# Decode attention with an MLP on one core: K transposed by VectorE in 32x32 blocks instead of by TensorE, and output sums spread over four quadrants

## The chip, the cores and the metric

The kernel runs on one core of a Trainium2 chip. Times are device microseconds of that core. The profile is one execution taken by the hardware profiler; its span is some 2 us shorter than the timed run.

## The reference

One decode step of four sequences: 32 query heads over 16 K/V heads, the last 2048 positions of the cache, and an MLP block on the same input, all added up.

```python
B, Sq, D = x.shape                    # 4, 1, 576
Hq, Dh = 32, 128
Hkv, Sk = k_cache.shape[1], k_cache.shape[2]     # 16, 8192
W = min(4096, max(256, Sk // 4))      # 2048
q = (x @ wq).reshape(B, Sq, Hq, Dh).transpose(0, 2, 1, 3)
k = jnp.repeat(k_cache[:, :, Sk - W:, :], rep, axis=1)     # rep = 2
v = jnp.repeat(v_cache[:, :, Sk - W:, :], rep, axis=1)
p = softmax(einsum("bhqd,bhkd->bhqk", q, k) * Dh ** -0.5)
o = einsum("bhqk,bhkd->bhqd", p, v)
attention = o.transpose(...).reshape(B, Sq, Hq * Dh) @ wo
# second branch; with one position the shifted h is zero, so x1 = x:
mlp = x + gelu(layernorm(x) @ w3) @ w4
# x above is the layernorm of the input; output: input + attention + mlp
```

What matters is the traffic: K and V of 16 heads are 2 MB each, with the weights 87.2 MB in all, and every byte is used once.

## The kernel before

All four sequences of one K/V head are one tile: partition p*4+b holds 64 consecutive positions of sequence b. TensorE transposes K in 128x128 chunks (64 per head), ScalarE and VectorE evict them (copy them from PSUM to SBUF), and each chunk then gives scores for the 8 queries of its head. Columns of the other sequences are masked.

```python
kvp = ...tile_pool(name="kv", bufs=NKV)             # NKV = 7, loads of K and V in one order
ps_tp, ps_s: 2 PSUM buffers each; ps_o, ps_m, ps_acc: 1
accB = AB[0:B, 448:448 + NB_]                       # 64 columns
accA = accA_t[0:B, :]                               # 512 columns, partitions 0 to 3
# ... cuts ...
def acc_matmuls(lhsT, rhs):                         # used by o_proj and mlp_out
    nc.tensor.matmul(out=accA, lhsT=lhsT, rhs=rhs[:, 0:NA], start=first, ...)
    nc.tensor.matmul(out=accB, lhsT=lhsT, rhs=rhs[:, NA:D], start=False, ...)

def k_transpose(h, g):                              # g: eight groups of 8 chunks
    tp = ps_tp.tile([P, GC, P], BF16, tag="tp")
    for i in range(GC):
        nc.tensor.transpose(out=tp[:, i, :], in_=kn[:, g * GC + i, :], identity=ident_bf[:])
    # ScalarE (g in 0,2,3,5,6) or VectorE copies tp to kt in SBUF

def k_scores(h, g):
    for i in range(GC):
        nc.tensor.matmul(out=S_ps[h][:, g * GC + i, :], lhsT=kt[:, i, :], rhs=q, start=True, stop=True)

# softmax of a head, one head behind the scores:
#   sm_max    VectorE maximum over the free axis of S
#   sm_maxT   TensorE transpose of it, mask, maximum, diagonal
#   sm_sub    "shift": TensorE spreads the maximum over all partitions; VectorE subtracts: T = S - m
#   sm_exp    one ScalarE exponential of 128 x 512
#   sm_den    VectorE sum of 128 x 512;  sm_rden: TensorE sum over partitions, reciprocal
def pv(h, g):                                       # two heads behind (LAG = 2)
    for c in range(g * GC, (g + 1) * GC):
        nc.tensor.matmul(out=o, lhsT=vn[:, c, :], rhs=PT[h][:, c, :], ...)

for t in range(Hkv + LAG + 1):                      # one step per head
    for g in range(NGR):
        k_transpose(t, g); k_scores(...); pv(t - LAG, g); o_proj(t - LAG - 1)  # and the softmax of t - 1
        # at t == 7: mlp_g, 180 matmuls
for lo, hi in zip(W4_PIECES, W4_PIECES[1:]):
    mlp_out(lo, hi)                                 # 36 "output steps", w4 is loaded last
```

## Time and profile before

| | |
|---|---|
| time, median of 3 runs | 241.27 us (237.99 to 242.65) |
| span of the profiled run (which took 240.92 us) | 239.1 us |
| TensorE busy | 189.5 us (79%) |
| VectorE / ScalarE busy | 95.9 / 55.8 us |
| loaded | 87.2 MB, at about 420 GB/s while it flows |

First the page of the kernel before. The first line below gives busy time, share and instructions of each engine; the others cut the span into 40 slices, with the busy tenths of TensorE, the TensorE clock that the profile shows as granted (9 is 90% or more) and the DMA engines' share.

```profile
PE 189.5 (79%) x3641; PEld 167.9 (70%) x3641; DVE 95.9 (40%) x226; ACT 55.8 (23%) x98; POOL 2.4 (1%) x12
...
PE   0544996999922492999997999989799998894994
...
PEclk9999999569975587696555556999869999955589
DMA  6999999999999999999999969999999999980000
```

The loads flow for 36 slices of 6 us and then stop; the last four slices, some 24 us, are a tail of TensorE work. So two things matter: how long the loads take, and what still has to be done when they end.

The groups of the kernel before: line, engine, operation, result and operands, shapes, count, then busy us and the mean ns of one.

```profile
L235 PE MATMUL tp<-ident_bf,kn 128*128 128x128 bf16 x1024 | 95.2, 248 | 10.8 <-DMA kn<-in_A_k_cache_dram 8.7
...
L240 ACT COPY kt<-tp 128x512 f32<-128x512 f32 x80 | 46.8, 586 | 149.2 <-PE tp L235 149.1
L242 DVE COPY kt<-tp 128x512 int32<-128x512 int32 x48 | 32.9, 686 | 63.8 <-PE tp L235 62.1
...
L286 DVE TENSOR_REDUCE dp<-pt 128x8 f32<-128x512 bf16 x16 | 17.4, 1090 | 15.1 <-ACT pt L281 15.1
```

K's transposes are the largest group of TensorE. A busy share of 79% does not say that they set the time: the timeline has to show that.

The timeline of the kernel before (start, duration, engine, line, operation), cut to the shift matmul of head 14, the projections of two heads and two of the output steps. Each output step is a pair, 512 columns and 64.

```profile
202.61 0.38 PE L222 MATMUL accA_t<-wo_sb,on 128*4 128x512 bf16 x1
...
202.85 0.38 PE L222 MATMUL accA_t<-wo_sb,on 128*4 128x512 bf16 x1
...
207.74 0.38 PE L271 MATMUL mb<-dg,ones_f 8*128 8x8 f32 x2
...
224.82 0.61 PE L222 MATMUL accA_t<-w_sb,gT 128*4 128x512 bf16 x1
...
225.30 0.61 PE L222 MATMUL accA_t<-w_sb,gT 128*4 128x512 bf16 x1
```

A step from 224.82 to 225.30 takes 0.48 us, twice the 0.24 us of the same shape at 202.6. The 576 columns of a step then pass at 1.2 per nanosecond instead of 2.4: TensorE runs at half its clock here.

### The profile page before, as it was taken

To read this page: it belongs to the slowest core of one execution; us is meant where nothing else is said; L and a number is where in the kernel's file an instruction comes from. 1 tells how busy PE (TensorE), PEld (TensorE's weight loads), DVE (VectorE), ACT (ScalarE), POOL (GpSimd) and SP (SyncE) were. 2 spreads that over 40 slices of the span, in tenths; PEclk is the share of its full clock that TensorE was granted. 3 is DMA by queue.
4 is the path that set the end of the run, shared out by engine and by line. 5 is a ranking of instruction groups with operands and counts; after the bars stand their busy time and mean duration, and the time that the engine had idled before them with its cause. 6 is when DMAs were issued, how large, how long until landed. Compare 5 with 4: busy or idle time off the path is not lost.

```text
span 239.1 us, 7840 instructions
## 1 busy us (share of the span) xinstructions
PE 189.5 (79%) x3641; PEld 167.9 (70%) x3641; DVE 95.9 (40%) x226; ACT 55.8 (23%) x98; POOL 2.4 (1%) x12
## 2 busy tenths in 40 slices
PE   0544996999922492999997999989799998894994
PEld 0433986988921392889996998888788987873441
DVE  5024264536530052352324444564425656544001
ACT  2000352324300041130021131342223433211000
POOL 3000000000000000000000000000000000000000
PEclk9999999569975587696555556999869999955589
DMA  6999999999999999999999969999999999980000
GB/s 234 422 436 433 392 419 425 411 426 423 434 417 419 423 394 425 425 423 419 433 419 391 426 255 430 397 408 422 407 401 423 425 433 410 419 349 8 3 0 2
DMA packets 10688, 87.67 MB, mean 367 GB/s; under 512 B 792, under 2 KB 4896, under 8 KB 5408
## 3 DMA queue, kind: packets, MB, share of 16 engines
q1 hardware_dynamic: 10656, 87.18, 88.1%
q8 instruction: 28, 0.46, 0.8%
q14 instruction: 4, 0.03, 0.0%
HBM read 87.17 MB, written 0.00 MB: 365 GB/s over the span
## 4 chain that ended last, share of the span: by engine, by line
PE 47%; DMA 39%; DVE 7%; issue 3%; ACT 2%; SPq 0%; DVEq 0%
DMA vn<-in_A_v_cache_dram 28%; PE tp L235 17%; DMA kn<-in_A_k_cache_dram 8%; PE accA_t L222 8%; PE O L302 6%; PE S L251 5%; PE AB L323 4%; DMA wq_sb<-in_A_wq_dram 3%; DVE dp L286 2%; PE mb L271 2%; PE dn L291 2%; ACT pt L281 1%; PE AB L223 1%; ACT kt L240 1%; DVE junk L262 1%
## 5 line engine op out<-in xcount | busy, mean ns | idle before, releaser
L235 PE MATMUL tp<-ident_bf,kn 128*128 128x128 bf16 x1024 | 95.2, 248 | 10.8 <-DMA kn<-in_A_k_cache_dram 8.7
L235 PEld LDWEIGHTS <-kn 128*128 128x128 bf16 x1024 | 74.4, 113 | 16.5 <-DMA kn<-in_A_k_cache_dram 9.0
L240 ACT COPY kt<-tp 128x512 f32<-128x512 f32 x80 | 46.8, 586 | 149.2 <-PE tp L235 149.1
L242 DVE COPY kt<-tp 128x512 int32<-128x512 int32 x48 | 32.9, 686 | 63.8 <-PE tp L235 62.1
L302 PE MATMUL O<-pt,vn 128*128 128x8 bf16 x1024 | 43.6, 167 | 13.9 <-DMA vn<-in_A_v_cache_dram 9.2
L251 PE MATMUL S<-qT,kt 128*128 128x8 bf16 x1024 | 46.3, 169 | 0.0
L302 PEld LDWEIGHTS <-vn 128*128 128x128 bf16 x1024 | 35.3, 99 | 15.1 <-DMA vn<-in_A_v_cache_dram 9.4
L251 PEld LDWEIGHTS <-kt 128*128 128x128 bf16 x1024 | 43.5, 102 | 0.5 <-issue 0.5
L286 DVE TENSOR_REDUCE dp<-pt 128x8 f32<-128x512 bf16 x16 | 17.4, 1090 | 15.1 <-ACT pt L281 15.1
L222 PE MATMUL accA_t<-wo_sb,on 128*4 128x512 bf16 x32 | 14.1, 503 | 0.3 <-DVE on L308 0.3
L262 DVE TENSOR_TENSOR junk<-mxT,maskT 8x128 f32<-8x128 f32 x16 | 4.5, 278 | 22.3 <-PE mxT L260 22.3
L323 PE MATMUL AB<-ln2T,w_sb 128*128 128x4 bf16 x144 | 11.8, 202 | 0.0
L323 PEld LDWEIGHTS <-w_sb 128*128 128x128 bf16 x144 | 11.6, 163 | 0.3 <-issue 0.2
L281 ACT ACTIVATE pt<-T 128x512 bf16<-128x512 f32 x16 | 10.1, 632 | 7.2 <-DVE T L275 7.2
L255 DVE TENSOR_REDUCE mx<-S 128x8 f32<-128x512 f32 x16 | 10.9, 682 | 1.9 <-PE S L251 1.9
L275 DVE TENSOR_TENSOR T<-S,mm 128x512 f32<-128x512 f32 x16 | 11.1, 692 | 0.5
L222 PE MATMUL accA_t<-w_sb,gT 128*4 128x512 bf16 x36 | 11.0, 438 | 0.0
L291 PE MATMUL dn<-dp,ones_f 128*128 128x8 f32 x32 | 7.3, 302 | 4.5 <-DVE dp L286 4.4
L291 PEld LDWEIGHTS dn<-dp,ones_f 128*128 128x128 f32 x32 | 6.0, 234 | 5.3 <-DVE dp L286 5.3
L271 PE MATMUL mb<-dg,ones_f 8*128 8x8 f32 x32 | 6.9, 287 | 2.2 <-DVE dg L266 1.1
L222 PEld LDWEIGHTS <-gT 128*4 128x4 bf16 x36 | 3.5, 96 | 6.4 <-issue 3.0
L271 PEld LDWEIGHTS mb<-dg,ones_f 8*128 8x128 f32 x32 | 5.5, 213 | 3.3 <-DVE dg L266 2.8
(67 smaller groups left out, 85.4 us busy)
## 6 DMA issues: line engine op xcount, KB each, us to landing
kn<-in_A_k_cache_dram SPq DMA_DIRECT2D x16, 2048.0 KB, 20.9
vn<-in_A_v_cache_dram SPq DMA_DIRECT2D x16, 2048.0 KB, 15.1
wo_sb<-in_A_wo_dram SPq DMA_DIRECT2D x4, 1152.0 KB, 28.0
w_sb<-in_B_w_dram SPq DMA_DIRECT2D x2, 2304.0 KB, 33.3
wq_sb<-in_A_wq_dram SPq DMA_DIRECT2D x4, 1024.0 KB, 8.9
w_sb<-in_B_w_dram SPq DMA_DIRECT2D x3, 1296.0 KB, 17.5
w_sb<-in_B_w_dram SPq DMA_DIRECT2D x2, 576.0 KB, 29.9
w_sb<-in_B_w_dram SPq DMA_DIRECT2D x1, 720.0 KB
```

The source lines that it names most:

```text
L222: nc.tensor.matmul(out=accA, lhsT=lhsT, rhs=rhs[:, 0:NA], start=first, stop=False, skip_group_check=True)
L235: nc.tensor.transpose(out=tp[:, i, :], in_=kn[:, g * GC + i, :], identity=ident_bf[:])
L240: nc.scalar.copy(out=d32.bitcast(F32), in_=s32.bitcast(F32))
L242: nc.vector.tensor_copy(out=d32.bitcast(I32), in_=s32.bitcast(I32))
L251: nc.tensor.matmul(out=S_ps[h][:, g * GC + i, :], lhsT=kt[:, i, :], rhs=q, start=True, stop=True)
L271: nc.tensor.matmul(out=mb[:], lhsT=ones_f[0:NJ, :], rhs=st[h][:], start=True, stop=True)
L275: nc.vector.tensor_tensor(out=T[:], in0=S_ps.pop(h)[:], in1=mm[:].unsqueeze(1).to_broadcast([P, NC, NJ]), op=ALU.subtract)
L281: nc.scalar.activation(out=pt[:], in_=st.pop(h)[:], func=ACT.Exp, scale=scale)
L286: nc.vector.reduce_sum(out=dp[:], in_=PT[h][:].rearrange("p c j -> p j c"), axis=AX.X)
L291: nc.tensor.matmul(out=dn[:], lhsT=ones_f[:], rhs=st.pop(("den", h))[:], start=True, stop=True)
L302: nc.tensor.matmul(out=o, lhsT=vn[:, c, :], rhs=PT[h][:, c, :], start=(c == 0), stop=(c == NC - 1))
L323: nc.tensor.matmul(out=g_ps[:, i, :], lhsT=w3[:, j * F + e * (F // 2) + f0:j * F + (e + 1) * (F // 2):NFH], rhs=ln2T[:, j, :], start=False ...
```

## The change

The intent is to free TensorE of K's transposes and their evictions. VectorE transposes K directly from SBUF to SBUF, in 32x32 blocks of 4-byte elements (pairs of bf16). A block transpose leaves the four quadrants of 32 partitions where they are, so one score matmul now handles four chunks at once against block-diagonal queries of 32 columns, once for each half and each element of the pair. The mask and the negative maximum are added into the score bank by two matmuls of 512 columns. The exponentials, straight from PSUM, also move the weights into the right quadrant: 16 small ones per head, one for each pair of reading and writing quadrant. The denominator becomes a matmul with ones. Independently of all that, the sums of the output are spread over four quadrants of 144 columns.

The core of the diff (pools, set-up of the queries and the loop are cut):

```diff
-    accB = AB[0:B, 448:448 + NB_]
-    accA_t = ps_acc.tile([P, NA], F32)
+    acc = ps_acc.tile([P, CW], F32)                      # CW = 144
     def acc_matmuls(lhsT, rhs):
-        nc.tensor.matmul(out=accA, lhsT=lhsT, rhs=rhs[:, 0:NA], start=first, ...)
-        nc.tensor.matmul(out=accB, lhsT=lhsT, rhs=rhs[:, NA:D], start=False, ...)
+        for i in range(NQD):                             # 4 quadrants
+            nc.tensor.matmul(out=acc[i * QD:i * QD + B, :], lhsT=lhsT, rhs=rhs[:, i * CW:(i + 1) * CW], ...)
-    def k_transpose(h, g):                               # 8 TensorE transposes and a copy, 8 times a head
+    def k_transpose(h, s):                               # 4 times a head
+        src = kv_tiles["K", h][:].bitcast(I32)[:, s * SC:(s + 1) * SC, :].rearrange("p c (ib i) -> p ib c i", i=QD)
+        kt = ktp.tile([P, 2, SC, QD], I32, tag="kt")
+        nc.vector.transpose(out=kt[:], in_=src)
+    def k_mask(h):
+        S_ps[h] = ps_s.tile([P, CG, NQD, NJ], F32, tag="S", name="S")      # bufs=2, one bank each
+        nc.tensor.matmul(out=S_ps[h]..., lhsT=ohT[:], rhs=nb, start=True, stop=False, ...)      # 512 columns
     def k_scores(h, s):
+        for g in range(SC // NQD):
+            for ie in range(4):
+                ib, e = divmod(ie, 2)
+                nc.tensor.matmul(out=S_ps[h][:, s * (SC // NQD) + g]...,
+                                 lhsT=kt[:, ib, g * NQD:(g + 1) * NQD, e:2 * QD:2]..., rhs=qz[:, h, ib, e]..., ...)
     def sm_sub(h):
-        # spread the maximum, then VectorE: T = S - m
+        nc.tensor.matmul(out=S_ps[h]..., lhsT=ones_bf[0:NJ, :], rhs=dg, start=False, ...)       # 512 columns
-    def sm_exp(h):
-        nc.scalar.activation(out=pt[:], in_=st.pop(h)[:], func=ACT.Exp, scale=scale)
+    def sm_exp(h, c4):
+        for kb in range(NQD):
+            nc.scalar.activation(out=PT[h][kb * QD:(kb + 1) * QD, :, c4, :],
+                                 in_=S_ps[h][c4 * QD:(c4 + 1) * QD, :, kb, :], func=ACT.Exp, scale=scale)
+    # pv: besides V, 8 matmuls with ones for the denominator
+    # order of a step, s = 0..3: transpose(t, s), [mask(t) at s = 0], scores(t, s),
+    #   softmax of t - 1 (s = 0: max, 1: maxT, 2: shift and exponentials), pv(t - 2, s), [o_proj(t - 3) at s = 0]
```

More of the change, by code (lines that the diff above doesn't have):

```diff
@@ L52 @@
     NJ = B * rep
-    GC = 8
-    NGR = NC // GC
-    NA = 512
-    NB_ = D - NA
-    assert NC * NJ <= 512 and NC % GC == 0
+    QD = 32
+    NQD = P // QD
+    CG = NC // NQD
+    NSL = 4
+    SC = NC // NSL
+    CW = D // NQD
+    DG = 8
+    assert NC * NJ <= 512 and SC % NQD == 0 and NC % DG == 0
     scale = float(Dh) ** -0.5
@@ L72 @@
     kvp = ctx.enter_context(tc.tile_pool(name="kv", bufs=NKV))
-    ktp = ctx.enter_context(tc.tile_pool(name="kt", bufs=4))
+    ktp = ctx.enter_context(tc.tile_pool(name="kt", bufs=3))
     ptp = ctx.enter_context(tc.tile_pool(name="pt", bufs=3))
-    tsp = ctx.enter_context(tc.tile_pool(name="ts", bufs=1))
     wp = ctx.enter_context(tc.tile_pool(name="w", bufs=1))
     wop = ctx.enter_context(tc.tile_pool(name="wo", bufs=2))
-    ps_tp = ctx.enter_context(tc.tile_pool(name="ps_tp", bufs=2, space=PSUM))
     ps_s = ctx.enter_context(tc.tile_pool(name="ps_s", bufs=2, space=PSUM))
-    ps_o = ctx.enter_context(tc.tile_pool(name="ps_o", bufs=1, space=PSUM))
+    ps_o = ctx.enter_context(tc.tile_pool(name="ps_o", bufs=2, space=PSUM))
     ps_m = ctx.enter_context(tc.tile_pool(name="ps_m", bufs=1, space=PSUM))
@@ L134 @@
     make_identity(nc, ident_f[:])
-    ones_f = const.tile([P, P], F32)
-    nc.gpsimd.memset(ones_f[:], 1.0)
+    ones_bf = const.tile([P, P], BF16)
+    nc.gpsimd.memset(ones_bf[:], 1.0)
     neg_half = const.tile([B, 1], F32)
@@ L143 @@
     g_ps = AB[:, Hq * B:Hq * B + NF * B].rearrange("p (f b) -> p f b", b=B)
-    accB = AB[0:B, 448:448 + NB_]
-    accA_t = ps_acc.tile([P, NA], F32)
-    accA = accA_t[0:B, :]
+    acc = ps_acc.tile([P, CW], F32)
+    nc.vector.memset(acc[:], 0.0)
     def layernorm(dst_f, dst_bf, src):
@@ L191 @@
                          rhs=xnT[:, KJ + e, :], start=False, stop=False, skip_group_check=True)
-    qT = const.tile([P, Hkv, B, rep], BF16)
-    nc.vector.tensor_copy(out=qT[:].rearrange("p h b r -> p h r b"),
-                          in_=q_ps.rearrange("p (h r) b -> p h r b", r=rep))
+    q_bf = const.tile([P, Hq * B], BF16)
+    nc.vector.tensor_copy(out=q_bf[:], in_=AB[:, 0:Hq * B])
+    sel = const.tile([P, 2, 2, NQD, QD], BF16)
+    for kb in range(NQD):
+        nc.vector.tensor_copy(out=sel[:, :, :, kb, :],
+                              in_=ident_bf[:].rearrange("p (ib i e) -> p ib e i", ib=2, e=2))
@@ new lines @@
+    qs_ps = ps_m.tile([P, 2, 2, Hkv, rep, B], F32, tag="m")
+    for ib in range(2):
+        for e in range(2):
+            nc.tensor.matmul(out=qs_ps[:, ib, e].rearrange("p h r b -> p (h r b)"),
+                             lhsT=sel[:, ib, e].rearrange("p k i -> p (k i)"), rhs=q_bf[:], start=True, stop=True)
+    qz = const.tile([P, Hkv, 2, 2, NQD, B, rep], BF16)
+    nc.gpsimd.memset(qz[:], 0.0)
+    for kb in range(NQD):
+        for ie in range(4):
+            ib, e = divmod(ie, 2)
+            nc.vector.tensor_copy(out=qz[kb * QD:(kb + 1) * QD, :, ib, e, kb, :, :],
+                                  in_=qs_ps[kb * QD:(kb + 1) * QD, ib, e].rearrange("p h r b -> p h b r"))
@@ L197 @@
     oh = const.tile([P, B], F32)
     nc.vector.reduce_sum(out=oh[:], in_=ident_f[:].rearrange("p (q b) -> p b q", b=B), axis=AX.X)
-    mask = const.tile([P, B, rep], F32)
+    oh_ps = ps_m.tile([B, P], F32, tag="m")
+    nc.tensor.transpose(out=oh_ps[:], in_=oh[:], identity=ident_f[:])
+    ohT = const.tile([B, P], BF16)
+    nc.vector.tensor_copy(out=ohT[:], in_=oh_ps[:])
+    negbig = const.tile([B, B, rep], BF16)
     for r in range(rep):
-        nc.vector.tensor_scalar(out=mask[:, :, r], in0=oh[:], scalar1=-1.0, scalar2=BIG,
+        nc.vector.tensor_scalar(out=negbig[:, :, r], in0=ident_f[0:B, 0:B], scalar1=-1.0, scalar2=BIG,
@@ L202 @@
                                 op0=ALU.add, op1=ALU.mult)
-    mask_f = mask[:].rearrange("p b r -> p (b r)")
-    mk_ps = ps_m.tile([NJ, P], F32, tag="m")
-    nc.tensor.transpose(out=mk_ps[:], in_=mask_f, identity=ident_f[:])
-    maskT = const.tile([NJ, P], F32)
-    nc.vector.tensor_copy(out=maskT[:], in_=mk_ps[:])
     xsum = const.tile([B, D], F32)
     nc.vector.tensor_tensor(out=xsum[:], in0=xn_f[:], in1=x_bf[:], op=ALU.add)
+    for i in range(NQD):
+        nc.tensor.matmul(out=acc[i * QD:i * QD + B, :], lhsT=ident_f[0:B, 0:B], rhs=xsum[:, i * CW:(i + 1) * CW],
+                         start=False, stop=False, skip_group_check=True)
@@ L214 @@
     gT = const.tile([P, NF, B], BF16)
-    acc_n = {"n": 0}
     def acc_matmuls(lhsT, rhs):
-        first = acc_n["n"] == 0
-        acc_n["n"] += 1
-        nc.tensor.matmul(out=accA, lhsT=lhsT, rhs=rhs[:, 0:NA], start=first, stop=False, skip_group_check=True)
-        nc.tensor.matmul(out=accB, lhsT=lhsT, rhs=rhs[:, NA:D], start=False, stop=False, skip_group_check=True)
+        for i in range(NQD):
+            nc.tensor.matmul(out=acc[i * QD:i * QD + B, :], lhsT=lhsT, rhs=rhs[:, i * CW:(i + 1) * CW],
+                             start=False, stop=False, skip_group_check=True)
     kts = {}
@@ L229 @@
     st = {}
-    def k_transpose(h, g):
-        kn = kv_tiles["K", h]
-        tp = ps_tp.tile([P, GC, P], BF16, tag="tp")
-        for i in range(GC):
-            nc.tensor.transpose(out=tp[:, i, :], in_=kn[:, g * GC + i, :], identity=ident_bf[:])
-        kt = ktp.tile([P, GC, P], BF16, tag="kt")
-        d32 = kt[:].rearrange("p a b -> p (a b)")
-        s32 = tp[:].rearrange("p a b -> p (a b)")
-        if g % 8 in (0, 2, 3, 5, 6):
-            nc.scalar.copy(out=d32.bitcast(F32), in_=s32.bitcast(F32))
-        else:
-            nc.vector.tensor_copy(out=d32.bitcast(I32), in_=s32.bitcast(I32))
-        kts[h, g] = kt
@@ L245, in k_scores @@
-    def k_scores(h, g):
-        if g == 0:
-            S_ps[h] = ps_s.tile([P, NC, NJ], F32, tag="S", name="S")
-        kt = kts.pop((h, g))
-        q = qT[:, h, :, :].rearrange("p b r -> p (b r)")
-        for i in range(GC):
-            nc.tensor.matmul(out=S_ps[h][:, g * GC + i, :], lhsT=kt[:, i, :], rhs=q, start=True, stop=True)
+    def k_transpose(h, s):
+        src = kv_tiles["K", h][:].bitcast(I32)[:, s * SC:(s + 1) * SC, :].rearrange("p c (ib i) -> p ib c i", i=QD)
+        kt = ktp.tile([P, 2, SC, QD], I32, tag="kt")
+        nc.vector.transpose(out=kt[:], in_=src)
+        kts[h, s] = kt
@@ new lines, in k_mask, with k_scores @@
+    def k_mask(h):
+        S_ps[h] = ps_s.tile([P, CG, NQD, NJ], F32, tag="S", name="S")
+        nb = negbig[:].rearrange("p b r -> p (b r)").unsqueeze(1).to_broadcast([B, CG * NQD, NJ])
+        nc.tensor.matmul(out=S_ps[h][:].rearrange("p g k j -> p (g k) j"), lhsT=ohT[:], rhs=nb,
+                         start=True, stop=False, skip_group_check=True)
+    def k_scores(h, s):
+        kt = kts.pop((h, s))[:].bitcast(BF16)
+        for g in range(SC // NQD):
+            for ie in range(4):
+                ib, e = divmod(ie, 2)
+                nc.tensor.matmul(out=S_ps[h][:, s * (SC // NQD) + g].rearrange("p k j -> p (k j)"),
+                                 lhsT=kt[:, ib, g * NQD:(g + 1) * NQD, e:2 * QD:2].rearrange("p c k -> p (c k)"),
+                                 rhs=qz[:, h, ib, e].rearrange("p k b r -> p (k b r)"),
+                                 start=False, stop=False, skip_group_check=True)
@@ L253, in sm_max @@
     def sm_max(h):
         mx = small.tile([P, NJ], F32, tag="mx")
-        nc.vector.reduce_max(out=mx[:], in_=S_ps[h][:].rearrange("p c j -> p j c"), axis=AX.X)
+        nc.vector.reduce_max(out=mx[:], in_=S_ps[h][:].rearrange("p g k j -> p j (g k)"), axis=AX.X)
         st[h] = mx
@@ L260, in sm_maxT @@
         nc.tensor.transpose(out=mxT[:], in_=st[h][:], identity=ident_f[:])
-        junk = small.tile([NJ, P], F32, tag="junk")
-        nc.vector.tensor_tensor(out=junk[:], in0=mxT[:], in1=maskT[:], op=ALU.add)
         m = small.tile([NJ, 1], F32, tag="m8")
-        nc.vector.reduce_max(out=m[:], in_=junk[:], axis=AX.X)
-        dg = small.tile([NJ, NJ], F32, tag="dg")
-        nc.vector.tensor_scalar_mul(out=dg[:], in0=ident_f[0:NJ, 0:NJ], scalar1=m[:, 0:1])
+        nc.vector.reduce_max(out=m[:], in_=mxT[:], axis=AX.X)
@@ L267, in sm_maxT @@
+        dg = small.tile([NJ, NJ], BF16, tag="dg")
+        nc.vector.tensor_scalar(out=dg[:], in0=ident_f[0:NJ, 0:NJ], scalar1=m[:, 0:1], scalar2=-1.0,
+                                op0=ALU.mult, op1=ALU.mult)
         st[h] = dg
     def sm_sub(h):
-        mb = ps_m.tile([P, NJ], F32, tag="m", name="mb")
-        nc.tensor.matmul(out=mb[:], lhsT=ones_f[0:NJ, :], rhs=st[h][:], start=True, stop=True)
-        mm = small.tile([P, NJ], F32, tag="mm")
-        nc.vector.tensor_tensor(out=mm[:], in0=mb[:], in1=mask_f, op=ALU.subtract)
@@ L274, in sm_sub @@
-        T = tsp.tile([P, NC, NJ], F32, tag="T")
-        nc.vector.tensor_tensor(out=T[:], in0=S_ps.pop(h)[:], in1=mm[:].unsqueeze(1).to_broadcast([P, NC, NJ]),
-                                op=ALU.subtract)
-        st[h] = T
-    def sm_exp(h):
-        pt = ptp.tile([P, NC, NJ], BF16, tag="pt")
-        nc.scalar.activation(out=pt[:], in_=st.pop(h)[:], func=ACT.Exp, scale=scale)
-        PT[h] = pt
-    def sm_den(h):
-        dp = small.tile([P, NJ], F32, tag="dp")
-        nc.vector.reduce_sum(out=dp[:], in_=PT[h][:].rearrange("p c j -> p j c"), axis=AX.X)
-        st["den", h] = dp
@@ L289, in sm_rden @@
-    def sm_rden(h):
-        dn = ps_m.tile([P, NJ], F32, tag="m", name="dn")
-        nc.tensor.matmul(out=dn[:], lhsT=ones_f[:], rhs=st.pop(("den", h))[:], start=True, stop=True)
-        rd = small.tile([P, NJ], F32, tag="rd", bufs=3)
-        nc.vector.reciprocal(out=rd[:], in_=dn[:])
-        st["rd", h] = rd
-    def pv(h, g):
-        if g == 0:
-            O_ps[h] = ps_o.tile([P, B, rep], F32, tag="O", name="O")
-        vn = kv_tiles["V", h]
-        o = O_ps[h][:].rearrange("p b r -> p (b r)")
-        for c in range(g * GC, (g + 1) * GC):
-            nc.tensor.matmul(out=o, lhsT=vn[:, c, :], rhs=PT[h][:, c, :], start=(c == 0), stop=(c == NC - 1))
-        if g == NGR - 1:
+        dg = st.pop(h)[:].unsqueeze(1).to_broadcast([NJ, CG * NQD, NJ])
@@ new lines, in sm_sub @@
+        nc.tensor.matmul(out=S_ps[h][:].rearrange("p g k j -> p (g k) j"), lhsT=ones_bf[0:NJ, :], rhs=dg,
+                         start=False, stop=False, skip_group_check=True)
+    def sm_exp(h, c4):
+        if c4 == 0:
+            PT[h] = ptp.tile([P, CG, NQD, NJ], BF16, tag="pt", name="pt")
+        for kb in range(NQD):
+            nc.scalar.activation(out=PT[h][kb * QD:(kb + 1) * QD, :, c4, :],
+                                 in_=S_ps[h][c4 * QD:(c4 + 1) * QD, :, kb, :], func=ACT.Exp, scale=scale)
+        if c4 == NQD - 1:
+            S_ps.pop(h)
@@ new lines, in pv @@
+    def pv(h, s):
+        if s == 0:
+            O_ps[h] = ps_o.tile([P, NJ + DG * NJ], F32, tag="O", name="O")
+        vn = kv_tiles["V", h]
+        pt = PT[h][:].rearrange("p g c j -> p (g c) j")
+        for c in range(s * SC, (s + 1) * SC):
+            nc.tensor.matmul(out=O_ps[h][:, 0:NJ], lhsT=vn[:, c, :], rhs=pt[:, c, :], start=(c == 0), stop=False,
+                             skip_group_check=True)
+        for c in range(s * SC, (s + 1) * SC, DG):
+            nc.tensor.matmul(out=O_ps[h][:, NJ:], lhsT=ones_bf[:],
+                             rhs=pt[:, c:c + DG, :].rearrange("p c j -> p (c j)"), start=False, stop=False,
+                             skip_group_check=True)
+        if s == NSL - 1:
@@ L304, in pv @@
             PT.pop(h)
     def o_norm(h):
+        o = O_ps.pop(h)
+        dn = small.tile([P, NJ], F32, tag="dn")
+        nc.vector.reduce_sum(out=dn[:], in_=o[:, NJ:].rearrange("p (c j) -> p j c", j=NJ), axis=AX.X)
+        rd = small.tile([P, NJ], F32, tag="rd")
+        nc.vector.reciprocal(out=rd[:], in_=dn[:])
         on = small.tile([P, rep, B], BF16, tag="on")
-        nc.vector.tensor_tensor(out=on[:].rearrange("p r b -> p b r"), in0=O_ps.pop(h)[:],
-                                in1=st.pop(("rd", h))[:].rearrange("p (b r) -> p b r", r=rep), op=ALU.mult)
+        nc.vector.tensor_tensor(out=on[:].rearrange("p r b -> p b r"), in0=o[:, 0:NJ].rearrange("p (b r) -> p b r", r=rep),
+                                in1=rd[:].rearrange("p (b r) -> p b r", r=rep), op=ALU.mult)
@@ L370 @@
     for t in range(Hkv + LAG + 1):
-        for g in range(NGR):
+        hm = t - 1
+        hv = t - LAG
+        for s in range(NSL):
             if t < Hkv:
-                k_transpose(t, g)
-            hs, gs = divmod(t * NGR + g - 2, NGR)
-            if 0 <= hs < Hkv:
-                k_scores(hs, gs)
-            hv = t - LAG
-            if 0 <= hv - 1 < Hkv and g == 0:
-                o_norm(hv - 1)
+                k_transpose(t, s)
+                if s == 0:
+                    k_mask(t)
+                k_scores(t, s)
+            if 0 <= hv - 1 < Hkv and s == 0:
+                o_norm(hv - 1)
+            if 0 <= hm < Hkv:
+                if s == 0:
+                    sm_max(hm)
+                elif s == 1:
+                    sm_maxT(hm)
+                elif s == 2:
+                    sm_sub(hm)
+                    sm_exp(hm, 0)
+                    sm_exp(hm, 1)
+                else:
+                    sm_exp(hm, 2)
+                    sm_exp(hm, 3)
             if 0 <= hv < Hkv:
-                pv(hv, g)
-            if 0 <= hv - 1 < Hkv and g == 0:
+                pv(hv, s)
+            if 0 <= hv - 1 < Hkv and s == 0:
                 o_proj(hv - 1)
-            hm = t - 1
-            if 0 <= hm < Hkv:
-                if g == 1:
-                    sm_max(hm)
-                elif g == 3:
-                    sm_maxT(hm)
-                elif g == 4:
-                    sm_sub(hm)
-                elif g == 5:
-                    sm_exp(hm)
-                elif g == 6:
-                    sm_den(hm)
-                elif g == 7:
-                    sm_rden(hm)
             if t == G_AT:
-                mlp_g(g * NF // NGR, (g + 1) * NF // NGR)
-                if g == NGR - 1:
+                mlp_g(s * NF // NSL, (s + 1) * NF // NSL)
+                if s == NSL - 1:
                     mlp_act()
@@ L403 @@
             pos["free"] += 1
-        if 0 <= t - LAG < Hkv:
+        if 0 <= hv < Hkv:
             pos["free"] += 1
@@ L408 @@
         mlp_out(lo, hi)
-    fin = const.tile([B, D], out.dtype)
-    nc.vector.tensor_tensor(out=fin[:, 0:NA], in0=accA, in1=xsum[:, 0:NA], op=ALU.add)
-    nc.vector.tensor_tensor(out=fin[:, NA:D], in0=accB, in1=xsum[:, NA:D], op=ALU.add)
-    nc.sync.dma_start(out=o2, in_=fin[:])
+    fin = const.tile([P, CW], out.dtype)
+    nc.vector.tensor_copy(out=fin[:], in_=acc[:])
+    for i in range(NQD):
+        eng = nc.sync if i % 2 == 0 else nc.scalar
+        eng.dma_start(out=o2[:, i * CW:(i + 1) * CW], in_=fin[i * QD:i * QD + B, :])
 _INS = ['A_x', 'A_k_cache', 'A_v_cache', 'A_wq', 'A_wo', 'B_x', 'B_w1', 'B_w2', 'B_w3', 'B_w4']
```

## The prediction

> **What bounds the kernel now.** The page has DMA at 9 tenths in almost every slice up to 215 us; 87.2 MB at about 420 GB/s (the stretch table) needs some 208 us. Two things keep the span at 239.1 us. First, TensorE lags the loads after the MLP step: the one-per-head shift matmuls (timeline) start at 117.2, then 137.0, then on average every 10.1 us (8.8 to 9 when the clock is granted, about 11 at half clock) to 207.7 for head 14. Second, a tail of 25 us follows the last load: softmax of head 15, its V product, then 36 output steps from 224.8 to 235.9, and the store. The chain of waits is DMA to about 96 us and mostly TensorE after it (transposes 17% of the span, output projections 8%).
>
> **Removed.** 1024 TensorE transposes (95.2 us busy by the groups; 0.61 to 1.01 us per eight), 1024 score pairs become 1024 of width 32; 128 evictions (ACT 46.8, VectorE 32.9); the shift subtraction (11.1), the denominator reduction (17.4) and the fp32 ones products on VectorE and TensorE.
>
> **Added.** 64 VectorE transposes of 1024 four-byte elements. The Trainium skill (Vector Engine (DVE) Microarchitecture Reference, section 3.8) gives one element per cycle and lane; no run here shows it. The 512-element reduction took 682 ns, so my estimate is 1.2 us each, 77 us in all, 4.8 per head. 256 small exponentials, 16 per head: 144 elements took 323 ns, 512 took 632, so about 280 each; the skill (ScalarE: Activation LUTs, "What ACT_TABLE_LOAD costs") says back-to-back ones overlap by about 93 ns, and the trace agrees (0.54 us from the start of a 632 ns one to the next). So 3.1 us per head if changes of quadrant do not stop the overlap, 4.5 if they do. Mask and shift: two 512-column matmuls per head. Weight loads of the scores now step by two elements: between the 25 to 33 ns per pair of the contiguous ones and the 62 ns of the strided MLP ones. Query set-up adds about 5 us before head 0, hidden behind the wait for V0.
>
> **Critical path.** TensorE work per head falls to about 7 us, but a loop appears: shift matmul 0.5, sixteen exponentials 3.6, mask of the next head but one (its score bank is the one being read) 0.4, scores 0.7, V product 0.6, projection 0.4, scores 0.7, maximum to the shift diagonal 0.8, VectorE transpose 1.3, scores 0.7: about 9.7 us per head, no faster than the DMA's 10. So most of the freed TensorE time is off the path. The MLP step stays (180 matmuls, 11 us). I expect the shift of head 7 near 133, of head 14 near 201 (207.7 before). The tail from there shrinks from 31 to about 24 us, mainly because the four quadrant outputs stream together (11 us becomes 6). Span near 225.
>
> **Prediction: 227 us**, 8 in 10 between 218 and 240. Faster by over 2%: 0.82; within 2%: 0.13; slower: 0.05.
>
> **What would show it.** Transposes near 1.2 us and VectorE busy near 120 us; ACT busy 60 to 75 us, with TensorE idle before the first V product waiting on exponentials; 9 to 11 us between shift matmuls; DMA near 9 tenths to about 212 us; output steps at 0.12 to 0.2 us instead of 0.3.
>
> **What would make it wrong.** Four-byte transposes at half rate (2.3 us) lift the head to over 12 us and cancel the gain. Exponentials that overlap and fast stepped weight loads bring it to the DMA's pace: about 219. Quadrant outputs that do not overlap give back 5 us. A TensorE clock stuck at half for long idle gaps costs some more.

## More of the kernel before

The kernel before has an uneven time: 28 timed runs of it in this study lie between 235.2 and 246.0 us, spread rather than in two groups. A run is called fast when it lies within 1.5% of the fastest of its own rounds.

## The result

| | before | changed |
|---|---|---|
| time, median of 4 runs | 239.63 us (237.04 to 242.65) | 226.39 us (226.25 to 226.79) |
| span | 239.1 us | 224.6 us |
| TensorE / VectorE / ScalarE busy | 189.5 / 95.9 / 55.8 us | 121.2 / 114.6 / 70.3 us |

The ratio is 0.9524, with a 95% interval of 0.9489 to 0.9560. Ratios here are those of fast runs of the same rounds; they are not the ratio of the medians quoted, and differ by up to 0.3% from the ratio of the mean times of the fast runs (0.9534 here). By the record's rule (2%, with the interval) this result counts as faster. Of the experiments only e12_out_outer does; all the others count as unclear against so uneven a kernel before. So they are compared with the changed kernel's 226.39 us instead, mostly across rounds and chips: e4_t3_twice and e13_diagonal, whose edits turn out to cost nothing, repeat it on two chips (226.46 and 226.56 us).

The same lines of the page, for the changed kernel:

```profile
PE 121.2 (54%) x2861; PEld 93.1 (41%) x2861; DVE 114.6 (51%) x214; ACT 70.3 (31%) x258; POOL 4.1 (2%) x13
...
PE   0451454545474144475995547474755546475584
...
PEclk9999999999999999999999999999999999999999
DMA  6999999999999999999999999999999999999600
```

Nothing is busy for more than 54% of the span apart from DMA. The loads end near 211 us and the tail is 13 us. The clock row shows full clock throughout; the experiments come back to that row, which misleads here.

The groups of the changed kernel that answer to those shown of before:

```profile
L292 ACT ACTIVATE pt<-S 32x128 bf16<-32x128 f32 x256 | 68.7, 269 | 106.9 <-issue 65.0
L249 DVE STREAM_TRANSPOSE kt<-kn 128x1024 int32<-128x1024 int32 x64 | 75.7, 1213 | 9.2 <-DMA kn<-in_A_k_cache_dram 9.2
...
L263 PE MATMUL S<-qz,kt 128*128 128x32 bf16 x1024 | 39.0, 189 | 30.0 <-DVE kt L249 30.0
```

A transpose of 1024 four-byte elements takes 1.213 us, as estimated. The Trainium skill (Vector Engine (DVE) Microarchitecture Reference, section 3.8) gives one element per cycle and lane. The trace agrees in the scaling: against the 0.676 us of a VectorE reduction of 512 elements (10.8 us for 16), twice the elements take 0.54 us more, about 1.05 ns each, which leaves an estimated 0.14 us that does not grow with them.

Where the 14.5 us of span went is read from marks that both timelines have: the shift matmul of a head, the first output step, the final addition. The last two columns belong to experiments below, each of which has one half of the change. The profiled run of the kernel before (240.92 us) is some 3 us above the mean of its two fastest timed runs (237.5 us), so some 3 of the 14.5 us belong to its uneven time; the marks cannot say where. The run of e7 is the fastest of its four.

| mark (us) | before | changed | transposes part alone (e6) | output part alone (e7) |
|---|---|---|---|---|
| shift, head 6 | 117.2 | 112.8 | 113.2 | 115.9 |
| shift, head 7 (after the MLP step) | 137.0 | 129.5 | 129.8 | 134.5 |
| shift, head 14 | 207.7 | 201.4 | 206.6 | 204.5 |
| mean per head, 7 to 14 | 10.10 | 10.28 | 10.97 | 10.01 |
| shift, head 15 | 216.3 | 208.5 | 214.4 | 211.8 |
| first output step | 224.8 | 217.4 | 224.7 | 218.9 |
| final addition | 235.9 | 221.5 | 235.0 | 222.8 |
| end | 239.1 | 224.6 | 238.2 | 226.3 |

The changed kernel is 7.5 us ahead after the MLP step, gains nothing over the seven heads that follow (it loses 1.2 us), though TensorE is idle for much of that time, and gains 7.0 us over the output steps (11.1 to 4.1 us). The lead at the MLP step belongs mostly to the transposes: with them alone it is 7.2 us (e6), with the outputs alone 2.5 us (e7).

The timeline of the changed kernel over one head, cut to the pieces that follow one another; the next head repeats it 10.27 us later.

```profile
150.01 0.60 PE L285 MATMUL S<-dg,ones_bf 8*128 8x512 bf16 x1
...
150.69 4.47 ACT L292 ACTIVATE pt<-S 32x128 bf16<-32x128 f32 x16 [5.81 <-issue]
...
155.22 0.58 PE L255 MATMUL S<-negbig,ohT 4*128 4x512 bf16 x1 [3.00 <-ACT pt L292]
...
155.73 0.61 PE L263 MATMUL S<-qz,kt 128*128 128x32 bf16 x16
...
156.18 0.57 PE L303 MATMUL O<-pt,vn 128*128 128x8 bf16 x16
...
156.80 0.41 PE L237 MATMUL acc<-wo_sb,on 128*4 128x144 bf16 x8
...
157.15 0.61 PE L263 MATMUL S<-qz,kt 128*128 128x32 bf16 x16
...
157.59 0.37 PE L275 MATMUL mxT<-ident_f,mx 128*8 128x128 f32 x1
...
158.00 0.28 DVE L277 TENSOR_REDUCE m<-mxT 8x1 f32<-8x128 f32 x1 [3.33 <-PE mxT L275]
...
158.32 0.22 DVE L279 TENSOR_SCALAR dg<-ident_f,m 8x8 bf16<-8x8 f32 x1
158.46 3.48 DVE L249 STREAM_TRANSPOSE kt<-kn 128x1024 int32<-128x1024 int32 x3
...
159.74 0.61 PE L263 MATMUL S<-qz,kt 128*128 128x32 bf16 x16 [1.24 <-DVE kt L249]
...
160.28 0.60 PE L285 MATMUL S<-dg,ones_bf 8*128 8x512 bf16 x1
```

Read the start times downwards: shift, exponentials, mask, scores, V product, projection, scores, maximum, diagonal, transpose, scores, shift. It is a closed chain in which no engine is busy for long. TensorE stands still for 3.00 us until the exponentials are done: the mask of the next head but one goes into the bank that they read, and the V product behind it needs them too. What ScalarE "waits for" reads "issue" in the profile; the shift matmul that ended 0.08 us before is the true cause. For the same reason the chain of waits of this profile breaks off and accounts for only 12% of the span, so here the loop has to be read from the timeline.

The output steps of the changed kernel: 144 matmuls of 144 columns, four per step, in 4.05 us.

```profile
217.36 4.05 PE L237 MATMUL acc<-w_sb,gT 128*4 128x144 bf16 x144
```

### The profile page after: what moved, and what is told of

Its sections match the earlier page's. It is cut to its first block, busy times and chain, and to the rows that moved or that the text cites. A ratio compares the mean times of both kernels' runs of the same rounds, so it can differ in the third digit from the quotient of the medians.

```text
span 224.6 us, 6358 instructions
## 1 busy us (share of the span) xinstructions
PE 121.2 (54%) x2861; PEld 93.1 (41%) x2861; DVE 114.6 (51%) x214; ACT 70.3 (31%) x258; POOL 4.1 (2%) x13
## 5 line engine op out<-in xcount | busy, mean ns | idle before, releaser
L292 ACT ACTIVATE pt<-S 32x128 bf16<-32x128 f32 x256 | 68.7, 269 | 106.9 <-issue 65.0
L249 DVE STREAM_TRANSPOSE kt<-kn 128x1024 int32<-128x1024 int32 x64 | 75.7, 1213 | 9.2 <-DMA kn<-in_A_k_cache_dram 9.2
L263 PEld LDWEIGHTS <-kt 128*128 128x128 bf16 x1024 | 33.1, 105 | 83.9 <-DVE kt L249 45.5
L263 PE MATMUL S<-qz,kt 128*128 128x32 bf16 x1024 | 39.0, 189 | 30.0 <-DVE kt L249 30.0
L255 PE MATMUL S<-negbig,ohT 4*128 4x512 bf16 x16 | 9.3, 583 | 39.8 <-ACT pt L292 39.8
L306 PE MATMUL O<-pt,ones_bf 128*128 128x64 bf16 x128 | 17.1, 226 | 0.0
L334 PE MATMUL AB<-ln2T,w_sb 128*128 128x4 bf16 x144 | 11.5, 201 | 0.0
L270 DVE TENSOR_REDUCE mx<-S 128x8 f32<-128x512 f32 x16 | 10.8, 676 | 0.0
L285 PE MATMUL S<-dg,ones_bf 8*128 8x512 bf16 x16 | 9.6, 601 | 0.1
L306 PEld LDWEIGHTS <-ones_bf 128*128 128x128 bf16 x128 | 8.4, 104 | 0.0
L336 PE MATMUL AB<-ln2T,w_sb 128*128 128x4 bf16 x36 | 7.3, 202 | 0.0
L237 PE MATMUL acc<-wo_sb,on 128*4 128x144 bf16 x128 | 6.6, 302 | 0.8 <-DVE on L319 0.8
```

The lines of the kernel that those rows point to most:

```text
L237: nc.tensor.matmul(out=acc[i * QD:i * QD + B, :], lhsT=lhsT, rhs=rhs[:, i * CW:(i + 1) * CW], start=False, stop=False, skip_group_check=True)
L249: nc.vector.transpose(out=kt[:], in_=src)
L255: nc.tensor.matmul(out=S_ps[h][:].rearrange("p g k j -> p (g k) j"), lhsT=ohT[:], rhs=nb, start=True, stop=False, skip_group_check=True)
L263: nc.tensor.matmul(out=S_ps[h][:, s * (SC // NQD) + g].rearrange("p k j -> p (k j)"), lhsT=kt[:, ib, g * NQD:(g + 1) * NQD, e:2 * QD:2].re ...
L270: nc.vector.reduce_max(out=mx[:], in_=S_ps[h][:].rearrange("p g k j -> p j (g k)"), axis=AX.X)
L285: nc.tensor.matmul(out=S_ps[h][:].rearrange("p g k j -> p (g k) j"), lhsT=ones_bf[0:NJ, :], rhs=dg, start=False, stop=False, skip_group_ch ...
```

## The experiments

Theory: the head's pace is the loop above, so time freed on TensorE is worth nothing until the loop is shortened, and the gain comes from the outputs and the MLP step. Rivals: VectorE's 7 us per head, or the loads, set the pace; the gain comes from K's transposes leaving TensorE; it comes from the higher clock that the profile shows.

### e1_s3: a third score bank

```diff
-    ps_s = ctx.enter_context(tc.tile_pool(name="ps_s", bufs=2, space=PSUM))
+    ps_s = ctx.enter_context(tc.tile_pool(name="ps_s", bufs=3, space=PSUM))
```

> Edit: three score banks instead of two, nothing else. Loop theory (one head takes 10.28 us because shift, sixteen exponentials, mask, scores, V product, projection, scores, maximum, transpose and scores follow one another): mask (0.50 us) and first scores (0.42) need no longer wait for the exponentials, so 9.36 us between shift matmuls where no load is awaited; the shift of head 14 moves from 201.4 to between 194 and 198, time 219 to 222. Rival (VectorE's own work, four transposes of 1.2 us and its waits for the maximum, sets the pace): no change, 226.4, 10.3 us per head.

Measured: 222.13 us (221.77 to 222.41), ratio to before 0.9385 (0.9297 to 0.9472); the shift matmuls are 9.25 us apart from head 8 to head 12 (138.11 to 175.13), and that of head 14 is at 195.99. The mask and the first scores have left the loop, and their time with them; the time lies just past the expected upper end. Heads 13 and 14 then wait for V. The rival of VectorE's pace falls, and so does that of the loads for these heads: the same loads now let them pass every 9.25 us. Two shifts in a row (heads 9 and 10):

```profile
147.37 0.60 PE L285 MATMUL S<-dg,ones_bf 8*128 8x512 bf16 x1
...
156.62 0.60 PE L285 MATMUL S<-dg,ones_bf 8*128 8x512 bf16 x1
```

### e4_t3_twice and e5_t2_twice: the same cost outside and inside the loop

```diff
         nc.vector.transpose(out=kt[:], in_=src)
+        if s == 3:              # e5_t2_twice: s == 2
+            nc.vector.transpose(out=kt[:], in_=src)
```

> Edit: the fourth transpose of each head is done twice (the result is the same). It adds 1.16 us of VectorE work per head, 18.6 in all, outside the loop, in the shadow of the exponentials. Loop theory: 226 to 227.5 us, still 10.28 per head. Rival (VectorE's work sets the pace): 1.16 us more per head, about 237 to 245.

Measured: 226.46 us, 10.28 us per head. Sixteen more transposes of 1.2 us cost nothing.

```profile
149.89 0.60 PE L287 MATMUL S<-dg,ones_bf 8*128 8x512 bf16 x1
...
160.17 0.60 PE L287 MATMUL S<-dg,ones_bf 8*128 8x512 bf16 x1
```

> Edit: the third transpose of each head is done twice; it stands inside the loop, between the shift diagonal and the scores in front of the shift. Loop theory: 11.44 us per head from head 7 on instead of 10.28, so 8 to 11 us longer: 234 to 238. Theory that DMA alone sets the pace: no change.

Measured: 237.56 us, 11.55 us per head. The same sixteen transposes, one place earlier in each head, cost 11.2 us. This pair is the clearest evidence of the loop: VectorE has the same amount of work in both.

```profile
154.94 0.60 PE L287 MATMUL S<-dg,ones_bf 8*128 8x512 bf16 x1
...
166.49 0.60 PE L287 MATMUL S<-dg,ones_bf 8*128 8x512 bf16 x1
```

### e3_same_quadrant: why the exponentials do not overlap

```diff
-            nc.scalar.activation(out=PT[h][kb * QD:(kb + 1) * QD, :, c4, :],
+            nc.scalar.activation(out=PT[h][c4 * QD:(c4 + 1) * QD, :, kb, :],
                                  in_=S_ps[h][c4 * QD:(c4 + 1) * QD, :, kb, :], func=ACT.Exp, scale=scale)
```

> Edit: each exponential writes to the quadrant that it reads from, so that four in a row keep their quadrants (wrong result on purpose: the weights stand at the wrong keys). Theory: the change of quadrant from one to the next is what keeps the exponentials from overlapping; then four per head start 0.28 us after the last and twelve about 0.19, sixteen take 3.3 to 3.5 us instead of 4.47, and the time is 219 to 223. Rival (they do not overlap because they are small, or read PSUM): 4.4 to 4.5 us and 226.4.

Measured: 220.04 us, 8.85 us per head from head 8 to 12, sixteen exponentials in 3.05 us. The result passed the comparison with the reference although the weights are at the wrong keys: by the scales of the reference's inputs the scores should be so small that the weights of a head are nearly equal (argued, not measured). The comparison does not see such a mistake.

The chain of waits of this run lists the exponentials in fours. Each four takes 0.74 to 0.77 us, and the next starts 0.76 to 0.77 us after it:

```profile
156.11 0.74 ACT pt L292 x4
156.87 0.75 ACT pt L292 x4
157.63 0.76 ACT pt L292 x4
158.40 0.77 ACT pt L292 x4
```

Busy time in stretches of 0.02 us shows the rest. Within a four the exponentials start about 0.16 us apart and two are in flight for about 0.1 us at each change; between one four and the next there is no overlap, and the step is 0.28 us. So three steps of 0.16 and one of 0.28 per four. In the changed kernel all steps are 0.28 us.

### e13_diagonal and e12_out_outer: other orders of the same exponentials

```diff
-        for kb in range(NQD):
-            nc.scalar.activation(out=PT[h][kb * QD:(kb + 1) * QD, :, c4, :],
-                                 in_=S_ps[h][c4 * QD:(c4 + 1) * QD, :, kb, :], func=ACT.Exp, scale=scale)
+        for i in range(NQD):
+            kb = (i + c4) % NQD
+            nc.scalar.activation(out=PT[h][kb * QD:(kb + 1) * QD, :, i, :],
+                                 in_=S_ps[h][i * QD:(i + 1) * QD, :, kb, :], func=ACT.Exp, scale=scale)
+        # e12_out_outer:         out=PT[h][c4 * QD:(c4 + 1) * QD, :, i, :],
+        #                        in_=S_ps[h][i * QD:(i + 1) * QD, :, c4, :]
```

> Edit: the sixteen exponentials of a head in another order, nothing else: each one's reading and writing quadrants both move on by one, so that the distance between the two stays the same for four in a row (right result). Theory A (an exponential that crosses quadrants cannot overlap with its neighbour): only the first four overlap, sixteen take 4.1 to 4.4 us, time 225 to 226.5. Theory B (what costs is a change of the distance between reading and writing quadrant from one to the next): sixteen take 3.1 to 3.4 us and, as in the run with equal quadrants, 219.5 to 221.

Measured: 226.56 us, sixteen in 4.47 us. Both theories of that text fall: even the first four, which do not cross quadrants, did not overlap.

> Edit: the sixteen exponentials of a head with their two loops exchanged: four in a row write the same quadrant and read four different ones (right result). In the changed kernel the writing quadrant changed and the reading one stayed, and none overlapped. If only a change of the writing quadrant costs the overlap: sixteen take about 3.05 us, 8.9 us per head, 219.5 to 221. If a change of either costs it: 4.47 us, 10.28 per head, 226.4.

Measured: 226.01 us, sixteen in 4.46 us. A change of the reading quadrant alone costs the overlap as well. Together with the changed kernel (writing quadrant alone), the diagonal order (both) and the steps between fours above (both), this leaves one theory: any change of a start quadrant from one exponential to the next costs the overlap of about 0.1 us. The sixteen pairs of quadrants are all different, so no order of these instructions avoids it.

### e6_wide_out: the changed kernel without the output part

```diff
-    acc = ps_acc.tile([P, CW], F32)
-    nc.vector.memset(acc[:], 0.0)
+    accB = AB[0:B, 448:512]
+    accA_t = ps_acc.tile([P, NA], F32)
+    nc.vector.memset(accA_t[:], 0.0)
     def acc_matmuls(lhsT, rhs):
-        for i in range(NQD):
-            nc.tensor.matmul(out=acc[i * QD:i * QD + B, :], lhsT=lhsT, rhs=rhs[:, i * CW:(i + 1) * CW], ...)
+        nc.tensor.matmul(out=accA, lhsT=lhsT, rhs=rhs[:, 0:NA], start=False, ...)
+        nc.tensor.matmul(out=accB, lhsT=lhsT, rhs=rhs[:, NA:D], start=False, ...)
     # and no first addition, the final one as before
```

> Edit: the changed kernel with the outputs taken back to two accumulators of 512 and 64 columns in one quadrant. Theory (the four quadrant outputs stream together): an output step goes back from 0.11 to 0.24 us at the full clock (0.48 at half), so 36 steps take 8.6 instead of 4.05 us, the projection in the loop 0.14 us more per head, the final additions 0.5 more: 231 to 233 us. Rival (the tail shrank only because the clock is full now): at most 1 us longer, 226.4 to 227.5.

Measured: 239.89 us, 13.5 us longer than the changed kernel and 7 us past the expected range; ratio to before 1.0147 (0.998 to 1.0314), so no faster than the kernel before. The marks of the table above say where: 0.69 us more per head in the loop (10.97 against 10.28), so 5.2 us by head 14 and 5.9 by head 15, and 7.6 us from there to the final addition.

The cost in the loop is what half the clock gives: the projection of a head takes 1.05 us here (from its first line below to the scores at 192.47 us), against 0.35 us in the changed kernel. The expectation had used the full clock because the profile shows it.

```profile
191.42 0.58 PE L236 MATMUL accA_t<-wo_sb,on 128*4 128x512 bf16 x1
...
191.87 0.61 PE L236 MATMUL accA_t<-wo_sb,on 128*4 128x512 bf16 x1
```

Of the 7.6 us at the end, 1.4 come before the output steps, with the last two projections, and 6.2 in them. Half the clock explains little of these 6.2: only the first five of the 36 steps take 0.48 us, the rest 0.25, and 36 steps of 0.245 us would already take an estimated 4.8 us more than the 4.05 us of the changed kernel. Two output steps early and two late:

```profile
225.64 0.61 PE L236 MATMUL accA_t<-w_sb,gT 128*4 128x512 bf16 x1
...
226.12 0.61 PE L236 MATMUL accA_t<-w_sb,gT 128*4 128x512 bf16 x1
...
227.70 0.38 PE L236 MATMUL accA_t<-w_sb,gT 128*4 128x512 bf16 x1
...
227.95 0.38 PE L236 MATMUL accA_t<-w_sb,gT 128*4 128x512 bf16 x1
```

And the table by stretches, whose entry behind the bracketed counts is the granted clock, for the time before and after 227.1 us:

```profile
222.70:227.10 4.40, 3.65 (x24) 1.41 (x22) 0.59 (x3) 0.00 (x0) 0.00 (x0) 1.00 0.02 4
227.10:234.90 7.80, 7.80 (x64) 3.52 (x62) 0.00 (x0) 0.00 (x0) 0.00 (x0) 1.00 0.00 0
```

The steps take 0.48 us and then 0.25, and the profile shows clock 1.00 for both. In the kernel before, the stretch from 217 to 224.8 us, with projections of the same 0.48 us, is shown with 0.50. The durations decide: TensorE runs the changed kernel at half its clock almost throughout (a 512-column shift matmul takes 0.58 to 0.60 us in every head). This run speeds up only in a dense stretch at the end. The Trainium skill (TensorE: Matmul & The Clock Gate, Part 1) says that "the default state is throttled, and activity releases the throttle". That fits this tail, but not, by itself, the MLP step of the changed kernel: TensorE is busy there without a gap from 104 to 120 us, and the mask right after it still takes 0.60 us:

```profile
120.47 0.60 PE L255 MATMUL S<-negbig,ohT 4*128 4x512 bf16 x1
```

So what sets the clock stays open. That the row knows only the changes of clock that it recorded, and takes full clock before the first, would fit too; no run shows it. The rival that the gain comes from the higher clock that is shown falls: this run shows 0.999 and gains nothing.

### e7_before_quad_out: the kernel before with the output part alone

```diff
     def acc_matmuls(lhsT, rhs):
-        nc.tensor.matmul(out=accA, lhsT=lhsT, rhs=rhs[:, 0:NA], start=first, ...)
-        nc.tensor.matmul(out=accB, lhsT=lhsT, rhs=rhs[:, NA:D], start=False, ...)
+        for i in range(NQD):
+            nc.tensor.matmul(out=acc[i * QD:i * QD + B, :], lhsT=lhsT, rhs=rhs[:, i * CW:(i + 1) * CW], ...)
     # and accumulator, first addition and final copy as in the change
```

> Edit: the kernel before with the outputs over four quadrants alone. Theory (transposes on TensorE pull the granted clock down, and the quadrant outputs are worth some 6 us of tail by themselves): granted clock as in the kernel before (0.75 to 0.85), output steps 0.12 us or, in the stretch at half clock, up to 0.2, and 231 to 234 us. Rival (all of the gain comes from K's transposes leaving TensorE): over 237.

Measured: 230.28 us (three fast runs of 228.16 to 231.13, one of 237.56 at clock 0.658), ratio 0.9741 (0.956 to 0.992); the median is just below the expected range, and that all of the gain comes from K's transposes (over 237 us) falls. The output steps take 3.81 us instead of 11.1:

```profile
218.91 3.81 PE L226 MATMUL acc<-w_sb,gT 128*4 128x144 bf16 x144
```

By the means below this is the larger part of the gain, from a dozen lines of the change, though the interval of its ratio is wide. Means of the fast runs of one chip and set of rounds: before 236.4, output part alone 229.6, transposes part alone 239.9; the changed kernel has 226.4 from its own rounds, and was not run beside these. The parts do not add up: the output part is worth 6.8 us on the kernel before and 13.5 us on the changed one, in part because there the projection stands inside the loop (5.9 us of it by head 15). So on top of the output part the transposes bring 3.2 us.

### e8_dummy_t and e9_dummy_m: does the kind of TensorE work move the clock?

```diff
+    # and a PSUM pool ps_j of one bank
+            if 0 <= hv < Hkv and s == NSL - 1:
+                vd = kv_tiles["V", hv]
+                junk_ps = ps_j.tile([P, 4, P], BF16, tag="j", name="junk")      # e9_dummy_m: F32
+                for i in range(32):
+                    nc.tensor.transpose(out=junk_ps[:, (i % 4), :], in_=vd[:, i, :], identity=ident_bf[:])
+                    # e9_dummy_m: nc.tensor.matmul(out=junk_ps[:, (i % 4), :], lhsT=vd[:, i, :], rhs=ident_bf[:], ...)
```

> Edit: the changed kernel with 32 transposes per head on TensorE, of a V tile into an unused PSUM bank, put where TensorE is idle for 3 us behind the last V product. Theory (transposes on TensorE are what lets the clock fall): the granted clock falls below 0.95, to between 0.7 and 0.95, and the time rises by 1 to 6 us. Rival (the clock follows how busy TensorE is, not with what): the clock stays at 0.99 or more, as in the run with plain matmuls.

> Edit: as the last run, but the 32 are plain matmuls of the same tiles with the identity, into an fp32 bank. Theory: the clock stays at 0.99 or more and the time within 1 us of 226.4, for they fit into the idle stretch. Rival (more TensorE work of any kind lowers the clock): below 0.95 in both.

Measured: 230.37 and 230.82 us, clock shown 0.745 and 0.733. Transposes and plain matmuls act alike, so the theory about transposes falls. The rival is not shown either, for the shown clock cannot be trusted: with the extra work the projection of eight matmuls takes 0.30 us in the heads shown as slower, and 0.41 us in the changed kernel, shown as full. (The shift of these heads stays at 0.60 us in all but one or two, so TensorE is not faster throughout.)

The clock row of the run with dummy transposes, to be set against the row of nines above:

```profile
PEclk9999999998576656658558559676675858576959
```

So the row falls where TensorE gets faster, in part at least. Most of the extra 4 us has another place: the step from head 6 to head 7, where TensorE is the busy engine, takes 19.3 us in the first run and 20.0 in the second (16.6 in the changed kernel); the heads after it keep 10.0 us in the first run and 10.26 in the second.

### e10_s3_lag3 and e14_best: the loop opened

```diff
-    ps_s = ...bufs=2...
+    ps_s = ...bufs=3...
-    LAG = 2
+    LAG = 3
```

e14_best has the diagonal order of e13_diagonal as well, which is worth nothing.

> Edit: three score banks, and the V product one head later than before, so that neither the scores nor the V product stand behind the exponentials. Loop theory: no loop is left through the exponentials; the heads run at the pace of the loads (about 10 us) and catch up after the MLP step at less than 8 us; what remains is the last load (about 212 to 214 us) with a few output steps and the store: 217 to 220.5. Rival (something else paces the heads at 9.25): as the run with three banks alone, 222.

> Edit: both of the other two of this call together. Where the last load sets the end, the order of the exponentials should add at most 1.5 us: 217 to 220. This is the version that the experiments point to; it should beat the changed kernel (226.4) by 2.5 to 4%.

Measured: 220.54 and 220.64 us (220.59 to 220.66), both just past the upper end of what was expected; ratios to before 0.929 and 0.9293 (0.9171 to 0.9416). Heads 7 to 9 follow at 7.85 us (125.56, 133.41, 141.26 in the first run), so the pace of 9.25 us fell with the loop; then they wait for the loads of K. The output steps at the end wait for the last pieces of w4, one of which the timeline of the second run shows:

```profile
214.38 0.65 PE L237 MATMUL acc<-w_sb,gT 128*4 128x144 bf16 x16 [0.64 <-DMA w_sb<-in_B_w_dram]
...
215.08 0.31 DVE L422 CAST fin<-acc 128x144 bf16<-128x144 f32 x1 [7.89 <-PE acc L237]
```

These two versions are the fastest of the correct ones. The second beats both kernels, the changed one by 2.5% (220.6 against 226.4, of different rounds). Behind the last load it has four output steps, an addition and the store, so only the loads themselves are left.

## Why the prediction was right

The time (226.39 for 227) and most marks fit. It is worth checking term by term, for two errors cancelled.

| step of the prediction | predicted | measured |
|---|---|---|
| a VectorE transpose | 1.2 us | 1.213 us |
| shift of head 7 | 133 us | 129.5 us |
| pace of the loop | 9.7 us | 10.28 us |
| - sixteen exponentials | 3.6 us (3.1 or 4.5) | 4.53 us to the mask |
| - each group of scores (three in the loop) | 0.7 us | 0.44 to 0.55 us |
| - shift, mask | 0.5, 0.4 us | 0.68, 0.51 us |
| - V product, projection | 0.6, 0.4 us | 0.62, 0.35 us |
| - maximum to diagonal, transpose | 0.8, 1.3 us | 0.87, 1.28 us |
| shift of head 14 | 201 us | 201.4 us |
| from there to the end | 24 us | 23.2 us |
| output steps, 36 | 6 us | 4.05 us |

- That the freed TensorE time is mostly off the path was right: a loop through the exponentials takes its place, as e1, e4 and e5 show.
- The exponentials were the term most in error. The prediction split the difference between overlap and none; there was none, because the quadrants change (e3, e12, e13).
- The scores were sized too high. A weight load that steps by two elements cost nothing that shows: sixteen pairs start about 0.028 us apart (0.61 us in all, of which 0.19 is the last one's own).
- The pace was 0.6 us too low and head 7 came 3.5 us earlier than predicted; over seven heads the two cancel to 0.4 us. The prediction expected some 3 us of gain over these heads (68 us from 133 to 201, against 70.7 before) and 4 us before them; in fact 7.5 us came before them, and over them 1.2 us were lost. So the exact hit of head 14 is partly luck.
- The gain of the outputs was under-rated. The prediction names the 11 us that become 6, and does not see that the projection of each head, 0.96 us at half clock, sits in the loop (1.05 us there with its waits in e6): with the old outputs the whole transposes part brings nothing (e6). What "would cost some more", the half clock, was in fact the state of the kernel almost throughout, and the durations used in the estimate happened to be near it.
- That DMA would be near nine tenths to about 212 us, and VectorE busy near 120 and ScalarE 60 to 75, was right (211, 114.6, 70.3).

What stays open: what sets the clock and why the profile's row and the durations disagree in just this way, and why the kernel before varies by 4% while the changed one does not.

## What to carry to other kernels

Taking work off the busiest engine buys nothing in those stretches where the new order of work closes a loop through a latency; write the loop down from its durations before the change, and look for the one extra buffer or the one step of lag that opens it (here one PSUM bank and one head of lag, 6 us). When a change has two independent parts, run each alone: here a dozen lines about where four output rows are stored carry more of the gain than the rewrite of the transposes, which alone is no faster. And trust the duration of a known shape before the clock that a profile prints.

## What the Trainium skill lacked or had wrong

- ScalarE: Activation LUTs (What ACT_TABLE_LOAD costs) says that back-to-back ones overlap by about 93 ns, with no condition. Here 32x128 exponentials start 0.16 us apart while reading and writing quadrants stay the same, and 0.28 us apart, with no overlap, as soon as either changes (4.47 against 3.05 us for sixteen).
- TensorE: Matmul & The Clock Gate tells the cold and the warm clock apart by durations, which this case confirms (576 columns in 0.48 and 0.245 us), and warns that the recorded clock events have been seen to be unreliable on trn2. What it lacks is this form of it: a profile's granted clock can read 1.00 in both states, as it does in e6.
- The same page, in its table of weight-path modes, allows a step between weight columns without saying what it costs. A step of 2 elements cost nothing here (0.028 us per pair of load and matmul of 32 columns); the MLP's step of 18 elements takes 0.062 us per pair (five in 0.31 us).
- The same page, Part 3, measures three column tiles of 512 columns at 2.38 times the speed. It has no figure for four tiles with few columns; here four of 144 columns take 0.11 us per step, mostly at the slow clock (the mask and shift of that kernel take 0.58 to 0.60 us), against 0.48 (slow) or 0.245 us for 576 columns in one quadrant.
